# V weights loaded in two halves, a V sum split around transposes, and a tiny early read: the opening of an attention + GLU kernel

## Chip, cores and metric

One core of one Trainium2 chip. The metric is the device time of one execution in microseconds (us). A chip of its own was used for each group of experiments, with the kernel before timed beside them; times are compared within a group.

## The reference, cut to what matters

```python
xn = layernorm(x)                       # x: 2048 x 512
qkv = xn @ wqkv                         # 512 x 1536, 32 heads of 16
A = softmax(mask(q k^T / 4)) v @ wo     # causal, window of 256
B = ((xn @ w_gate) * (xn @ w_up)) @ w_down      # 512 -> 1792 -> 512
return x + A + B
```

## The kernel before

The change touches only the opening, before the steady stream of matmuls. `x` arrives in blocks of 128 rows; VectorE takes the statistics and scales a block (`xn`), TensorE transposes it (four 128 x 128 transposes into PSUM), ScalarE copies it to `xnT`, and four matmuls over the four parts of the 512 input rows make V for the block (`proj_v`). The first K/Q matmul follows when V is made for four blocks.

```python
for lo, hi in ((0, 1), (1, 2), (2, 4)):                 # x blocks 0, 1, 2-3
    nc.sync.dma_start(out=self.x[:, lo:hi, :], in_=xv[:, lo:hi, :])
for lo in (1024, 512, 0):                               # weights of V, K, Q
    nc.sync.dma_start(out=self.Wqkv[:, :, lo:lo + 512], in_=wq[:, :, lo:lo + 512])
# ... gate, up, down and output weights, the rest of x ...
self.keep_busy(40)                                      # filler matmuls, on zeros
# ... first_chunk():
self.norm_transpose(0, False)
self.keep_busy(8)
for b in range(4):
    if b < 3:
        self.norm_transpose(b + 1, False)
    self.proj_v(b, engine="act" if b == 2 else "dve")
    if b == 0:
        self.norm_apply(3)                              # scale block 3
self.proj_qk(0, 0, 1, engine="dve")                     # the first K/Q matmuls
```

The softmax here doesn't subtract the row's maximum and nothing guards it: scores larger than these inputs give would overflow.

## Time and profile before

| | |
|---|---|
| time, median of the first 3 runs | 264.87 us (264.74 to 264.91) |
| the run whose profile was taken | 265.39 us, span 263.7 us |
| TensorE busy | 259.4 us, 98% of the span |
| first V sum / first K/Q matmul | 7.26 / 11.35 us from the span's start |

The chain of work that ended last, as shares of the span, first by engine and then by line:

```profile
PE 96%; DMA 2%; SPq 0%; issue 0%; DVE 0%
PE gp L395 19%; PE up L406 19%; PE psd L428 17%; PE qkp L251 11%; PE S L312 10%; PE acc L366 6%; PE vp L239 5%; PE psd L434 5%; PE L L428 2%; DMA Wqkv<-in_A_wqkv_dram 2%; PE L L434 1%; PE L L366 0%; SPq L74 0%; PE xTp L209 0%; DVE x L444 0%
```

Everything on it is TensorE's work, but for 2% on the load of the V weights.

### The profile page before, as it was taken

The numbers are of one execution on the slowest core, as the hardware profiler recorded it, in microseconds if no ns is written. First come the engines' busy times: TensorE is split into PE (matmuls) and PEld (weight loads), VectorE is DVE, ScalarE is ACT, GpSimd is POOL, SyncE is SP. The second block draws the span as 40 slices with busy tenths as digits, with TensorE's granted clock in tenths as the row PEclk, the third lists the DMA queues.
The fourth block names the chain that finished last, engine by engine and source line by source line (L and its number), as shares of the span: only waits on it lengthen the run. The fifth ranks groups of instructions, "written<-read, shape, count | busy, mean of one in ns | idle before, by whom it ended". The sixth has DMA issues, their size and how long they took to land.

```text
span 263.7 us, 8896 instructions
## 1 busy us (share of the span) xinstructions
PE 259.4 (98%) x3890; PEld 120.9 (46%) x3890; DVE 175.1 (66%) x342; ACT 175.5 (67%) x141; POOL 116.9 (44%) x278
## 2 busy tenths in 40 slices
PE   8999999999999999999999999999999999999996
PEld 8444444444444544444544454444544445444453
DVE  6677888877845497567873669766685135977344
ACT  3376788888856866677776566767777546787600
POOL 6216342425457645334456644544453451463600
PEclk9999999999999999999999999999999999999999
DMA  6999921220002600002001310000100100000002
GB/s 180 378 357 340 281 29 22 24 47 4 0 25 57 84 2 0 4 0 47 5 0 42 81 45 2 0 2 19 32 4 0 42 21 22 5 0 2 4 2 80
DMA packets 19431, 15.12 MB, mean 57 GB/s; under 512 B 7360, under 2 KB 19392, under 8 KB 19392
## 3 DMA queue, kind: packets, MB, share of 16 engines
q1 hardware_dynamic: 18848, 14.26, 19.9%
q8 instruction: 30, 0.49, 0.8%
q10 hardware_dynamic: 544, 0.30, 0.4%
q14 instruction: 9, 0.07, 0.1%
HBM read 9.70 MB, written 2.10 MB: 45 GB/s over the span
## 4 chain that ended last, share of the span: by engine, by line
PE 96%; DMA 2%; SPq 0%; issue 0%; DVE 0%
PE gp L395 19%; PE up L406 19%; PE psd L428 17%; PE qkp L251 11%; PE S L312 10%; PE acc L366 6%; PE vp L239 5%; PE psd L434 5%; PE L L428 2%; DMA Wqkv<-in_A_wqkv_dram 2%; PE L L434 1%; PE L L366 0%; SPq L74 0%; PE xTp L209 0%; DVE x L444 0%
## 5 line engine op out<-in xcount | busy, mean ns | idle before, releaser
L319 ACT ACTIVATE P<-S 128x2048 bf16<-128x2048 f32 x75 | 140.7, 1876 | 50.6 <-PE S L312 46.8
L158 POOL TENSOR_SCALAR_AFFINE_SELECT P<-P 64x256 bf16<-64x256 bf16 x224 | 100.9, 450 | 126.3 <-ACT P L319 112.1
L395 PE MATMUL gp<-xnT,Wg 128*128 128x512 bf16 x224 | 60.1, 380 | 0.0
L406 PE MATMUL up<-xnT,Wu 128*128 128x512 bf16 x224 | 59.1, 380 | 0.0
L411 DVE TENSOR_TENSOR hT<-up,gsb 128x512 bf16<-128x512 f32 x56 | 38.3, 685 | 19.3 <-PE up L406 13.7
L428 PE MATMUL psd<-Wd,hT 128*128 128x512 bf16 (+1 forms) x210 | 48.0, 369 | 0.0
L343 DVE TENSOR_TENSOR P<-P,diag 128x512 bf16<-128x512 bf16 (+1 forms) x75 | 29.4, 392 | 6.1 <-ACT P L319 6.1
L428 PEld LDWEIGHTS <-hT 128*128 128x128 bf16 x238 | 21.3, 98 | 25.1 <-issue 2.9
L406 PEld LDWEIGHTS <-Wu 128*128 128x128 bf16 x224 | 20.5, 98 | 25.4 <-issue 2.5
L395 PEld LDWEIGHTS <-Wg 128*128 128x128 bf16 x224 | 20.3, 98 | 25.1 <-issue 1.9
L312 PE MATMUL S<-Q,K 16*64 16x320 bf16 (+4 forms) x720 | 31.0, 260 | 0.0
L312 PE MATMUL S<-Q,Ko 32*64 32x320 bf16 (+4 forms) x720 | 30.9, 260 | 0.0
L251 PE MATMUL qkp<-xnT,Wqkv 128*128 128x512 bf16 x128 | 29.9, 380 | 0.0
L230 ACT ACTIVATE gsb<-gp 128x512 bf16<-128x512 f32 x39 | 22.9, 596 | 8.2 <-PE gp L395 7.4
L312 PEld LDWEIGHTS <-K 16*64 16x64 bf16 x720 | 12.1, 103 | 30.7 <-issue 30.7
L372 DVE STREAM_TRANSPOSE at<-acc 128x512 f32<-128x512 f32 x30 | 19.1, 688 | 8.9 <-PE acc L366 8.9
L444 DVE TENSOR_TENSOR x<-psd,x 128x512 bf16<-128x512 f32 (+1 forms) x15 | 9.7, 655 | 15.7 <-PE psd L434 15.7
L251 PEld LDWEIGHTS <-Wqkv 128*128 128x128 bf16 x128 | 11.7, 98 | 14.5 <-issue 1.6
L366 PE MATMUL acc<-P,VS 64*32 64x320 bf16 (+4 forms) x672 | 17.7, 253 | 0.0
L366 PE MATMUL acc<-P,V 64*32 64x320 bf16 (+4 forms) x672 | 17.5, 253 | 0.0
L366 PEld LDWEIGHTS <-V 64*32 64x32 bf16 x720 | 15.1, 91 | 2.2 <-issue 1.6
L239 PE MATMUL vp<-Wqkv,xnT 128*128 128x512 bf16 x64 | 15.3, 380 | 0.5 <-DMA Wqkv<-in_A_wqkv_dram 0.5
(54 smaller groups left out, 200.2 us busy)
## 6 DMA issues: line engine op xcount, KB each, us to landing
out_dram<-x SPq DMA_DIRECT2D x15, 128.0 KB, 1.7
Wg<-in_B_w_gate_dram SPq DMA_DIRECT2D x2, 896.0 KB, 11.4
Wu<-in_B_w_up_dram SPq DMA_DIRECT2D x2, 896.0 KB, 13.7
Wd<-in_B_w_down_dram SPq DMA_DIRECT2D x1, 1792.0 KB, 17.2
Wqkv<-in_A_wqkv_dram SPq DMA_DIRECT2D x3, 512.0 KB, 5.9
x<-in_A_x_dram SPq DMA_DIRECT2D x2, 512.0 KB, 8.7
VS<-V SPq DMA_DIRECT2D x6, 144.0 KB, 2.6
x<-in_A_x_dram SPq DMA_DIRECT2D x3, 256.0 KB, 6.6
```

Source lines behind the costliest of these rows:

```text
L158: nc.gpsimd.affine_select(out=v, in_=v, pattern=pattern + [[1 if diag else -1, 64]], compare_op=ALU.is_ge if diag else ALU.is_gt, fill=0.0 ...
L230: nc.scalar.activation(out=out, in_=in_, func=ACT.Copy)
L239: nc.tensor.matmul(ps[:], lhsT=self.xnT[T][:, b, k, :], rhs=self.Wqkv[:, k, 1024:1536], start=(k == 0), stop=(k == 3))
L251: nc.tensor.matmul(ps[:], lhsT=self.Wqkv[:, k, lo:lo + 128], rhs=self.xnT[T][:, :, k, :], start=(k == 0), stop=(k == 3))
L312: nc.tensor.matmul(S[64 * par:64 * par + 64, e, col:col + n], lhsT=(self.Ko if par else self.K)[U, c][rows, keys], rhs=self.Q[T, c][rows, ...
L319: nc.scalar.activation(out=P[:, :, 0:col], in_=S[:, :, 0:col], func=ACT.Exp, scale=0.25)
L343: self.nc.vector.tensor_tensor(out=v, in0=v, op=ALU.min, in1=self.diag.unsqueeze(1).unsqueeze(1).to_broadcast([128, 4, n, 64]))
L366: nc.tensor.matmul(accs[par][32 * e:32 * e + 32, q:q + n], lhsT=v, rhs=P[rows, e, col:col + n], start=(i == 0), stop=(i == len(todo) - 1), ...
L395: nc.tensor.matmul(ps[:], lhsT=self.Wg[:, k, 128 * f:128 * f + 128], rhs=self.xnT[T][:, :, k, :], start=(k == 0), stop=(k == 3))
L406: nc.tensor.matmul(ps[:], lhsT=self.Wu[:, k, 128 * f:128 * f + 128], rhs=self.xnT[T][:, :, k, :], start=(k == 0), stop=(k == 3))
L411: nc.vector.tensor_tensor(out=self.hT[T, f][:], in0=ps[:], in1=self.gsb[:], op=ALU.mult)
L428: nc.tensor.matmul(ps, lhsT=self.hT[T, f][:, 128 * b:128 * b + 128], rhs=self.Wd[:, f, c0:c1], start=(f == 0), stop=False)
```

## The change

Its intent is to shorten TensorE's wait for the V weights: load them in two halves of input rows, begin block 0's sum with the first half, put block 1's transposes between its halves (`self.cur` holds the PSUM tile of the open sum), and touch the weights early with a 16 x 32 read. Two loads of later x blocks are merged with a third, and block 3 is scaled earlier.

```diff
-        for lo in (1024, 512, 0):
-            nc.sync.dma_start(out=self.Wqkv[:, :, lo:lo + 512], in_=wq[:, :, lo:lo + 512])
+        for lo, ks in ((1024, slice(0, 2)), (1024, slice(2, 4)), (512, slice(0, 4)), (0, slice(0, 4))):
+            nc.sync.dma_start(out=self.Wqkv[:, ks, lo:lo + 512], in_=wq[:, ks, lo:lo + 512])
-        for lo, hi in ((8, 10), (10, 12), (12, NT)):
+        for lo, hi in ((8, NT),):
+        first = const.tile([16, 32], BF16, name="first")
+        nc.scalar.dma_start(out=first[:], in_=self.w_d["qkv"][0:16, 1024:1056])
-        (nc.gpsimd if t else nc.vector).tensor_scalar(out=ve[:], ...
+        (nc.vector if t in (0, 3) else nc.gpsimd).tensor_scalar(out=ve[:], ...
-        for b in range(4):
-            if b < 3:
-                self.norm_transpose(b + 1, False)
-            self.proj_v(b, engine="act" if b == 2 else "dve")
-            if b == 0:
-                self.norm_apply(3)
+        self.proj_v(0, (0, 1))
+        first = self.cur
+        self.norm_transpose(1, False)
+        self.cur = first
+        self.proj_v(0, (2, 3), engine="act")
+        self.norm_apply(3)
+        self.proj_v(1, (0, 1))
+        self.norm_transpose(2, False)
+        self.proj_v(1, (2, 3), engine="dve")
+        self.norm_transpose(3, False)
+        self.proj_v(2, engine="act")
+        self.proj_v(3, engine="dve")
```

More of the change, by code (lines that the diff above doesn't have):

```diff
@@ L178, in norm_scale @@
         ve = self.small.tile([128, n], F32, tag="ve", name="ve")
-        (nc.gpsimd if t else nc.vector).tensor_scalar(out=ve[:], in0=mv[:, :, 1], scalar1=1e-5, scalar2=None,
+        (nc.vector if t in (0, 3) else nc.gpsimd).tensor_scalar(out=ve[:], in0=mv[:, :, 1], scalar1=1e-5, scalar2=None,
                                                       op0=ALU.add)
```

## The prediction

> **What bounds the kernel now.** I read the page's busy table first, then what TensorE waited for, then the chain that ended last over its first 12 us, then the timeline of single engines there.
>
> The busy table:
> ```profile
> PE 259.4 (98%) x3890; PEld 120.9 (46%) x3890; DVE 175.1 (66%) x342; ACT 175.5 (67%) x141; POOL 116.9 (44%) x278
> ```
> TensorE is busy for 259.4 of 263.7 us; the next engine has 67%. So TensorE's own work sets the time, and only idle time of TensorE can be won. All the waits of TensorE's matmuls in the whole span:
> ```profile
> PE wps L127 <- DVE idle L94: 1.1, 1, 1.1
> PE vp L239 <- DMA Wqkv<-in_A_wqkv_dram: 0.5, 1, 0.5
> ```
> There are two. The first is the start of the program. The second is the first V projection (`proj_v` of block 0), waiting for the V weights. After that, measured in the stretch 11.51 to 255 us, TensorE is busy 243.49 of 243.49 us. So whatever moves the first K/Q projection (the end of the opening) moves the end by as much, and nothing later can absorb it. The chain over the opening:
> ```profile
> 2.17 4.96 DMA Wqkv<-in_A_wqkv_dram
> 7.12 0.14 issue
> 7.26 1.02 PE vp L239 x4
> 8.28 0.22 PE xTp L209 x4
> 8.50 0.88 PE vp L239 x4
> 9.38 0.01 issue
> 9.39 0.40 PE xTp L209 x4
> 9.79 1.73 PE vp L239 x8
> 11.51 2.59 PE qkp L251 x12
> ```
> The load of the V weights (512 KB, 128 partitions) lands at 7.12 and TensorE goes on at 7.26. Then comes work without a gap, but for one small thing: the transposes of block 3 start at 9.39 while block 1's sum starts at 8.34 and needs 4 x 0.216 = 0.86 us of issue, so they could have started at 9.20. The reader sees the reason in two timeline lines: the block was scaled on VectorE only after the copy of V block 0.
> ```profile
> 8.93 0.40 DVE L190 TENSOR_SCALAR xn<-x,mv,rs 128x512 bf16<-128x512 bf16 x1
> 9.38 0.23 PEld L209 LDWEIGHTS <-xn 128*128 128x128 bf16 x4 [0.51 <-DVE xn L190]
> ```
> The last view is what else stands before the first V sum, TensorE and ScalarE:
> ```profile
> 5.74 0.76 PE L127 MATMUL wps<-idle 128*128 128x128 bf16 x8
> 6.35 0.40 PE L209 MATMUL xTp<-ident,xn 128*128 128x128 bf16 x4
> ```
> ```profile
> 5.77 0.66 ACT L210 ACTIVATE xnT<-xTp 128x256 bf16<-128x256 bf16 x2 [3.48 <-PE xTp L209]
> 6.78 0.60 ACT L210 ACTIVATE xnT<-xTp 128x512 bf16<-128x512 bf16 x1 [0.36 <-PE xTp L209]
> 9.82 0.60 ACT L210 ACTIVATE xnT<-xTp 128x512 bf16<-128x512 bf16 x1 [0.69 <-PE xTp L209]
> ```
> The 8 filler matmuls end their issue at 6.35. Block 0's transposed input is in SBUF in two pieces, at about 6.15 and 6.43. So, but for its weights, the first V sum could start at 6.35. The second ACT line is a cost that the present order hides: from the start of a block's transposes (6.35) to its copy (6.78) are 0.43 us, the copy takes 0.60, and from its end to the matmul that reads it pass some 0.05 us. That is **1.08 us from the start of a block's transposes to its V sum**. Before, block 1's round trip lies wholly under the wait for the weights.
>
> **What the Trainium skill says.** "DMA: Bandwidth & Descriptors", section "Why a DMA increments its semaphore by 16 and not by 1": each engine that takes part counts only after its own data, and only the full 16 means that all has landed. The trace agrees: of the V weights' 16 semaphore packets the first starts at 5.74, most by 6.26, the last at 6.74, and the landing is at 7.12; one slow engine holds the whole load. Same page, "Issuing engines are not separate DMA queues": transfers issued by ScalarE and SyncE share the same 16 engines and interleave. So the tiny read can't have a path of its own; before, no ScalarE transfer exists in the opening, so no run here shows it yet. "TensorE: Matmul & The Clock Gate", section "Wait — 56ns, not 53.3ns?": 215.7 ns from start to start for 512 columns at full clock and 55.6 for 128. The trace agrees: four V matmuls plus the next step take 8.118 - 7.257 = 0.861 us, and the four transposes 8.118 to 8.341 = 0.223.
>
> **The change part by part.**
>
> *Order.* Added TensorE work is nil: the same 16 V matmuls and 16 transposes, in the order V0 (rows 0, 1), transposes 1, V0 (rows 2, 3), V1 half, transposes 2, V1 half, transposes 3, V2, V3. After the opening the order of instructions is the same as before on every compute engine.
>
> *Half of the weights.* A half is 16 KB for each DMA engine instead of 32, in packets of 1 KB whose median is 46 ns. So each engine counts about 16 x 0.046 = 0.74 us earlier: the slowest at some 6.0 instead of 6.74, landing near 7.12 - 0.74 = 6.4, or sooner if the straggler's stall lay in the second half (the typical engine would count by 5.5, landing by 5.9). With the 0.14 us from landing to matmul, the first V sum starts between 6.35 (where the fillers hold it) and 6.54.
>
> *Tiny read.* In the packets the first ones of each load on an engine are slow: 0.25 us for x, up to 0.75 us around 4.3 us where the first of the V weights come, against 46 ns; the four-to-five stretch moves 176 GB/s against 388 in seven-to-eight. I take the intent to be to pay the weights' first access early. It can take up to about 0.5 us off the landing of the first half. But past 6.2 us of landing this wins nothing, since fillers and transposes then hold. Its price is 16 packets of 64 bytes on the engines that fetch x block 0, on which all the normalisation hangs (landed 2.87, statistics from 2.90). I put 0.05 us of delay there.
>
> *Sum, with the first V sum at t0 = 6.35.*
> - V0 half: 2 x 0.216 = 0.43, so transposes 1 start at 6.78 (0.43 later than before).
> - Transposes 1 take 0.22; V0's second half runs 7.00 to 7.44 if its weights have landed by about 6.9. Landed as late as before it runs 7.26 to 7.69, still hidden by the next step.
> - V1's first half needs block 1's copy: 6.78 + 1.08 = 7.86. So TensorE waits about 0.4 us here: the old wait comes back in part, on ScalarE.
> - V1 half to 8.29, transposes 2 from 8.29 to 8.51, V1's other half to 8.94, transposes 3 to 9.17. Block 3's scaling now needs no V copy and should end near 8.4, so the 0.18 us are gone.
> - V2 needs block 2's copy: 8.29 + 1.08 = 9.37 (ScalarE's copy of V0, about 7.9 to 8.5, is out of its way), so 0.2 us of wait. V2 and V3 take 8 x 0.216 = 1.73, to 11.10.
>
> K/Q starts at t0 + 4.75 = 11.10 instead of 11.35: **0.25 us won**. Adding 0.05 for x and 0.05 for a t0 between 6.35 and 6.54 leaves 0.15 to 0.2. So the half's earlier start of up to 0.9 us (7.26 to 6.35) is mostly given back, since block 1's transposes, which used to fill the wait, now stand behind half a sum and bring their round trip to light.
>
> *The rest.* The merged x load and the split of the weights keep the number of loads, and change only which earlier load a later one waits for; gate weights land at 12.49 and are used at 19.18, so nothing comes of it.
>
> **The rivals.**
> 1. *The tiny read holds up x block 0.* For: all share 16 engines, and the first access to the weights was the slowest seen (0.75 us). If it stands ahead of x on each engine and blocks, x lands up to 0.5 us later and every step moves: 264.87 - 0.25 + 0.5 = 265.1. Against: 64 bytes an engine, issued beside x and not before it.
> 2. *The first half lands no earlier than about 6.6*, because a stalled engine is late whatever its share. The break-even is t0 = 11.35 - 4.75 = 6.60; then the time stays at 264.87. For: the landing's tail (6.26 to 6.74) is made of stalls, not of bytes.
> 3. *The tiny read also speeds up x* (its first packets, 0.25 us, may be a start cost of the engines): up to 0.2 us more, 264.4. Against: nothing in the trace shows x waiting for more than its own first access.
> 4. *A large win of 0.9 us*, the whole wait gone and T3's delay too: 263.9. Against it is the 1.08 us round trip, which occurs twice on the new path (blocks 1 and 2).
>
> **Range and chances.** 264.87 - 0.2 = 264.65 us. The three runs of before lie within 0.17 us. Rival 1 gives the upper end, rival 3 with noise the lower: 264.25 to 265.0. A change of 2% is 5.3 us, while the whole opening holds 0.5 us of wait plus 0.18 us of late transposes, and a loss of 5 us would need something to break in a stretch whose order is the same. So within 2% has 0.99.
>
> **What would show it right or wrong.** Right: the first V sum starts near 6.4 with two matmuls, the V weights are gone from TensorE's waits and one for ScalarE's copy of block 1 of 0.2 to 0.4 us stands there; block 3's scaling ends before 8.6; the first K/Q matmul starts near 11.1 to 11.2; the rest of the timeline is moved by that difference. The tiny read's part shows in x block 0's landing (2.87 before) and in the packets around 4 us. Wrong: x lands after 3.1; the first V sum still waits for weights past 6.6; a load's new wait delays gate weights or the blocks of chunk 1; or K/Q starts well before 11.0, which would mean that the round trip is shorter than read here.

## The result, and the profile after

| | before | after |
|---|---|---|
| median of 6 runs | 264.85 us (264.73 to 265.43) | 265.25 us (264.74 to 265.44) |
| ratio after to before | | 1.0009, 95% interval 0.9995 to 1.0022 |
| the profiled run | 265.39 us | 265.20 us |
| first V sum / first K/Q | 7.26 / 11.35 us | 6.38 / 11.14 us |

A ratio here is the mean time of one kernel's fast runs over that of the other's of the same rounds, so it is not quite the ratio of the medians. Executions over 1.5% slower than the fastest of the same kernel are left out of the means. The class is "same"; a small loss is likelier than the gain of 0.2 us that was forecast, and 265.25 lies above the forecast range (264.25 to 265.0). Yet the two *profiles* differ as forecast: K/Q starts 0.21 us sooner. The busy line and the chain of the changed kernel:

```profile
PE 257.6 (98%) x3872; PEld 120.9 (46%) x3890; DVE 174.7 (66%) x342; ACT 176.0 (67%) x142; POOL 116.4 (44%) x277
...
PE 98%; issue 1%; ACT 0%; DVE 0%
```

The DMA share has gone from the chain. TensorE's busy time seems to fall by 1.8 us, but so does the count of its matmuls, by 18, while the count of weight loads is 3890 in both: those are records missing from the trace, not work saved. Profiles with all 3890 records (split2, split4) have none of the "issue" waits of the lines psd, vp and L below, so these come of the missing records too. What TensorE waited for in the changed kernel (line, cause, us in total, times, longest):

```profile
PE psd L436 <- issue: 1.1, 7, 0.2
PE wps L129 <- DVE idle L96: 1.1, 1, 1.1
PE vp L241 <- ACT xnT L212: 0.3, 1, 0.3
PE vp L241 <- issue: 0.2, 1, 0.2
PE L L436 <- issue: 0.2, 1, 0.2
```

The wait for the weights is replaced by one for ScalarE's copy of block 1, as forecast. Its timeline on TensorE and on ScalarE:

```profile
5.74 0.80 PE L129 MATMUL wps<-idle 128*128 128x128 bf16 x8
6.38 0.38 PE L241 MATMUL vp<-Wqkv,xnT 128*128 128x512 bf16 x1
6.81 0.39 PE L211 MATMUL xTp<-ident,xn 128*128 128x128 bf16 x4
7.03 0.59 PE L241 MATMUL vp<-Wqkv,xnT 128*128 128x512 bf16 x2
7.89 0.60 PE L241 MATMUL vp<-Wqkv,xnT 128*128 128x512 bf16 x2 [0.26 <-ACT xnT L212]
8.33 0.39 PE L211 MATMUL xTp<-ident,xn 128*128 128x128 bf16 x4
...
9.40 1.90 PE L241 MATMUL vp<-Wqkv,xnT 128*128 128x512 bf16 x8
11.14 2.75 PE L253 MATMUL qkp<-xnT,Wqkv 128*128 128x512 bf16 x12
```

```profile
7.23 0.60 ACT L212 ACTIVATE xnT<-xTp 128x512 bf16<-128x512 bf16 x1 [0.81 <-PE xTp L211]
```

From block 1's transposes (6.81) to its V sum (7.89) are the 1.08 us of the forecast; from t0 = 6.38 to K/Q (11.14) are 4.76 us against 4.75 forecast. So the mechanism of the forecast stood in this run (block 3's scaling ended at 8.62, a hair after the 8.6 named, and held nothing up), and the time did not follow. Either the profile of before was not of a typical run, or the gain was lost after the opening. The second is soon excluded: the last matmul starts 249.47 us after the first K/Q in both profiles (260.82 - 11.35 and 260.61 - 11.14), with no wait but the missing records. In nearly all later profiles, too, the time of the profiled run is the start of K/Q plus 254.0 to 254.2 us; the exceptions are few_fill (255.0) and both looks at split4 (254.3), and they are taken up below. So, but for these, **K/Q's start can be read for the time.** This also leaves nothing for the merged x load to explain, which was not tested alone.

### The profile page after: what moved, and what is told of

Same layout as the page of the kernel before. It is cut to its first block, busy times and chain, and to the rows that moved or that the text cites. A ratio compares the mean times of both kernels' runs of the same rounds, so it can differ in the third digit from the quotient of the medians.

```text
span 263.5 us, 8878 instructions
## 1 busy us (share of the span) xinstructions
PE 257.6 (98%) x3872; PEld 120.9 (46%) x3890; DVE 174.7 (66%) x342; ACT 176.0 (67%) x142; POOL 116.4 (44%) x277
## 4 chain that ended last, share of the span: by engine, by line
PE 98%; issue 1%; ACT 0%; DVE 0%
PE gp L403 19%; PE up L414 19%; PE psd L436 17%; PE qkp L253 11%; PE S L320 10%; PE acc L374 6%; PE vp L241 5%; PE psd L442 5%; PE L L436 2%; PE wps L129 2%; PE L L442 1%; PE xTp L211 0%; PE L L374 0%; ACT xnT L212 0%; DVE x L452 0%
## 5 line engine op out<-in xcount | busy, mean ns | idle before, releaser
L436 PE MATMUL psd<-Wd,hT 128*128 128x512 bf16 (+1 forms) x198 | 46.1, 368 | 1.4 <-issue 1.1
```

What stands on the lines that cost most here:

```text
L436: nc.tensor.matmul(ps, lhsT=self.hT[T, f][:, 128 * b:128 * b + 128], rhs=self.Wd[:, f, c0:c1], start=(f == 0), stop=False)
```

## The experiments

In each, an expectation stood before the run. The theories: **D**, the spread of run times comes from when the V weights land; **C**, it comes from when TensorE's clock is granted in full; **L**, the change pays only if weights are late; **B**, splitting a load delays its end; **F**, a loss through instruction fetches.

### b1 and b2: the kernel before again

No edit.

> The kernel before again, to see whether its profile above (span 263.7 us, run of 265.4 us) shows a typical run: five of its other six runs took 264.73 to 264.91 us, and one 265.43. Theory D (late DMA): the spread between about 264.8 and 265.4 comes from the landing of the V weights; a run of 264.8 us then has them landed near 6.5 us instead of 7.12 and its first K/Q matmul near 10.8 instead of 11.35. Theory C (clock): the spread comes from when TensorE's clock is granted in full (6.04 us in the profile above); a run of 264.8 us then has it at 5 us or sooner with the V weights still landing near 7.1. If this profile is again of a run of 265.4 us, it shows only that the landing repeats.

> A third look at the kernel before. If a landing of the V weights at 7.1 us is the exception that made the first profiled run take 265.4, this one has it at 6.4 to 6.8, K/Q at 10.7 to 10.95 and takes 264.7 to 265.0. If it again takes 265.3 or more, its K/Q starts near 11.35 with a landing near 7.1 or a clock granted later than 6.8 us.

Measured: b1 264.89 us (264.83 to 264.96; the kernel before beside it 264.95, 264.67 to 265.09 in 11 runs), b2 264.84 us. V weights landed at 6.57 and 6.45 us, K/Q at 10.88 and 10.75. TensorE's matmuls on b1:

```profile
5.74 0.99 PE L127 MATMUL wps<-idle 128*128 128x128 bf16 x8
6.57 0.39 PE L209 MATMUL xTp<-ident,xn 128*128 128x128 bf16 x4
6.79 1.03 PE L239 MATMUL vp<-Wqkv,xnT 128*128 128x512 bf16 x3
```

and on b2:

```profile
5.46 0.61 PE L127 MATMUL wps<-idle 128*128 128x128 bf16 x8
6.42 0.40 PE L209 MATMUL xTp<-ident,xn 128*128 128x128 bf16 x4 [0.34 <-DVE xn L190]
6.65 1.03 PE L239 MATMUL vp<-Wqkv,xnT 128*128 128x512 bf16 x3
```

Neither has a wait for the V weights at all. The chain of b2 in the opening, in order of time, shows what bounds a run whose clock comes early (4.79 us): VectorE's statistics and scaling of block 1, then its transposes.

```profile
5.17 0.61 DVE st L169
5.79 0.02 issue
5.81 0.18 DVE mv L170
5.99 0.38 DVE xn L190
6.37 0.05 issue
6.42 0.40 PE xTp L209 x4
```

So theory D holds for the first profile: its landing at 7.12 us was an exception, and it is the reason why that run took 265.39 us. The wait which the change attacks does not exist in the runs that make the median. Theory C is not dead, though. The 8 fillers took 0.61 us in b2 and 0.99 in b1, and in b1 their end, not VectorE, released block 1's transposes (they start at 6.57 instead of 6.42). The list of runs hints at C as well: of the 38 timed runs of the kernel before beside the experiments, the eight whose mean clock is listed as 0.999 took 265.06 to 265.22 us, the other thirty 264.65 to 265.11, and the one profiled run with 0.999, split2b, got its full clock late (6.74). That the clock makes this smaller spread is not shown.

### a1 and a2: the changed kernel again

No edit.

> The changed kernel again. Its profile (run of 265.2 us) starts the first V sum at 6.38 and K/Q at 11.14 with the clock granted at 6.13 us; two of its six runs took 264.74 and 264.80. Theory C: in a run of about 264.75 us the clock is granted before 5.3 us, the fillers and the transposes of block 0 run at full speed, and K/Q starts near 10.7. Theory D: the weights land at the same times in both kinds of run, since they land before they are needed (5.15 and 5.80 in the profile), so the spread of this kernel can't be the landing of the V weights. On the same chip as the kernel before I expect this one between 0.1 us faster and 0.4 us slower in the mean.

> A third look at the changed kernel. K/Q at the later of t0 + 4.75 and the second half's landing + 3.81; t0 is 5.98 with an early clock, 6.38 to 6.58 with a late one. So K/Q between 10.75 and 11.35, and a time of K/Q + 254.05 (from 264.96 and 10.92): 264.8 to 265.4.

Measured: a1 265.05 us (264.93 to 265.32), ratio 1.0006 (0.9994 to 1.0018); a2 265.15 us. K/Q at 10.92 and 11.07. With the clock granted early (4.28 and 4.95 us) the first V sum started at 5.98 and 5.99, but then the *second* half of the weights was late (7.20 and 7.36). Of the waits of a1, the two that no missing record made and that lie after the start:

```profile
PE vp L241 <- DMA Wqkv<-in_A_wqkv_dram: 0.4, 1, 0.4
PE xTp L211 <- DVE xn L192: 0.2, 1, 0.2
```

Theory D was wrong for this kernel in the form ("they land before they are needed"): its second half does hold it. The two bounds are t0 + 4.75 and the start of V0's second half + 3.67 (0.43 + 0.43 + 1.08 + 1.73): 7.24 + 3.67 = 10.91 for a1 and 7.40 + 3.67 = 11.07 for a2, as measured.

### noread: the change without the tiny read

```diff
-        first = const.tile([16, 32], BF16, name="first")
-        nc.scalar.dma_start(out=first[:], in_=self.w_d["qkv"][0:16, 1024:1056])
```

> The changed kernel without ScalarE's tiny read. If the read is what brought the V weights in early (second half landed at 5.80 against 7.12 us before), then without it the first half lands near 6.2 to 6.4 and the second near 7.1, V0's second half waits until 7.2, and K/Q stays near 11.1, since block 1's round trip through ScalarE ends the wait anyway: time within 0.15 us of the changed kernel. x block 0 lands near 2.87 instead of 2.99. If instead the split or chance brought them in early, the halves land near 5.2 and 5.8 here too.

Measured: 265.40 us (264.99 to 266.29), ratio 1.0021 (1.0009 to 1.0033). Halves landed at 6.13 and 7.41, x block 0 at 2.91. The fillers ran at half speed to their end (8 in 1.01 us), t0 was 6.58 and K/Q came at 11.34 = t0 + 4.76. The profiled run is thus explained without the read. The expectation of a time within 0.15 us of the changed kernel was missed (265.40 against a1's 265.05). Whether the runs are slower than the changed kernel's because of the read is left open: the two intervals overlap.

### order_old: the change's loads with the old order

```diff
-        self.proj_v(0, (0, 1))
-        # ... V0 and V1 in halves around the transposes of blocks 1, 2 ...
+        self.norm_apply(3)
+        for b in range(4):
+            if b < 3:
+                self.norm_transpose(b + 1, False)
+            self.proj_v(b, engine="act" if b == 2 else "dve")
```

> The changed kernel with its loads and its tiny read, but V0's sum whole and behind block 1's transposes as before (block 3 still scaled before V0's copy). If the V weights land by 5.8 us as in the changed kernel's profile, the transposes of block 1 start at 6.4, the first V sum at 6.6 without a wait for ScalarE, and K/Q at 10.5 to 10.6: 0.5 to 0.6 us before the changed kernel's 11.14 and the time 0.5 us less, near 264.3 to 264.8. If the early landing was chance and they land near 7.1, K/Q starts near 11.2, as in the kernel before less the 0.18 us of block 3.

Measured: 265.05 us (264.98 to 265.59), ratio 1.0010 (0.9998 to 1.0022); the hoped-for 0.5 us did not come. The second half landed at 7.84, V0's second half waited 0.55 us for it, and K/Q started at 11.35. The early landing of the first profile after (6.50) was not the rule: of nine profiles with two loads one other (few_fill, 6.58) came near it.

### b_late and a_late: weights made late on purpose

The load of x blocks 4 to 7 (512 KB) goes ahead of the V weights, in both kernels.

```diff
+        nc.sync.dma_start(out=self.x[:, 4:8, :], in_=xv[:, 4:8, :])
         for lo in (1024, 512, 0):        # a_late: the four loads of the change
         # ... in the loop over the gate and up weights, further down:
-            if lo == 0:
-                nc.sync.dma_start(out=self.x[:, 4:8, :], in_=xv[:, 4:8, :])
```

> The kernel before with the load of x blocks 4 to 7 (512 KB) moved ahead of the V weights, so that these land late in every run. Theory L (the change pays only when the V weights are late): from the profiles, K/Q in the kernel before starts 4.23 us after the landing of the V weights if these are what the first V sum waits for (7.12 gave 11.35). 512 KB at 380 GB/s are 1.4 us, so they land at 8.0 to 8.5, K/Q starts at 12.2 to 12.8, and the run takes 1.3 to 1.9 us more than the kernel before on the same chip. A rival, that the time before does not hang on the weights at all, says no change.

> The changed kernel with the same 512 KB ahead of the V weights. Theory L: K/Q starts at the later of t0 + 4.75 (t0 the start of the first V sum) and the landing of the second half + 3.81 (0.14 to the matmul, 0.43 V0's second half, 0.43 V1's first half, 1.08 block 2's round trip, 1.73 V2 and V3). With the second half landing at 8.0 to 8.8 that is 11.8 to 12.6, so about 0.4 us before the other late kernel if both have the same landing, and the run is 0.2 to 0.5 us faster than it. If the change is no better here either, the split itself (more stragglers, a later landing) costs what it saves.

Measured: b_late 269.05 us (266.51 to 269.96), ratio 1.0141 (1.0090 to 1.0193); a_late 267.06 us (266.03 to 270.18, the last one the slow run), ratio 1.0069 (1.0047 to 1.0091), beside 264.80 for the kernel before. The expected sizes were missed. The mean clock listed for each run tells much of the reason: three of b_late's four runs have 0.987 to 0.994 (3.41 us at half clock, as in the profile below, take 0.006 off the mean), and only 266.51 has 1.000; a_late's three runs at 1.000 took 266.03, 266.67 and 267.44. At an equal clock there is no gain from the change to be seen, though one run against three is little. The profiles say more. In b_late the weights landed at 8.83 and the first V sum started at 8.96, but K/Q only at 14.54, 1.5 us later than landing + 4.23. The stretches of TensorE below (length, us busy, number, granted clock, DMA share, GB/s) show why:

```profile
6.66:10.07 3.41, 1.46 (x15) 1.00 1.03 345
10.07:13.48 3.41, 3.41 (x15) 0.50 1.06 389
13.48:16.89 3.41, 3.41 (x17) 1.00 1.08 386
```

TensorE was busy for 1.46 of 3.41 us, and in the next 3.41 us its clock was halved. This is what the Trainium skill describes ("TensorE: Matmul & The Clock Gate", "What's actually happening"): the clock depends on how busy windows of some 3.4 us were, and the windows do not start with the kernel. The trace agrees to the hundredth: 3.41 us. In a_late TensorE stood idle for longer, 2.65 us at a stretch against 1.95, and kept its clock: the grant began at 4.11 there, so the wait fell into two windows, busy for 1.64 us (4.11 to 7.52) and 2.14 us (7.52 to 10.93).

In a_late the first half landed at 8.46 and the second at 9.56. K/Q started at 13.36, where landing + 3.81 says 13.37. But the split had cost more than it saved: with a landing at 8.83 and no loss of clock the old order would have reached 8.83 + 4.23 = 13.06. Theory L is not borne out: as far as these runs show, the lead of the late changed kernel is that of a clock which it happened to keep.

### few_fill: 3 fillers instead of 8 in the changed kernel

```diff
-        self.keep_busy(8)
+        self.keep_busy(3)
```

> The changed kernel with 3 filler matmuls instead of 8 between block 0's transposes and its first V sum. In the four profiles of this order the sum started at 6.38, 5.98, 6.58 and (old order) later, whenever the fillers were through: 107 ns each until the clock is granted in full, 56 after. Theory C (clock): the fillers hold t0; without five of them t0 is 6.2 (ScalarE's first piece at 6.15), K/Q starts near 10.95 to 11.0 whatever the clock does, 0.15 to 0.4 us sooner than in the runs with a late clock, and the time is 0.1 to 0.3 us less than the changed kernel's, with the second half of the weights as the next bound (landing + 3.81). Rival: fewer fillers leave TensorE less busy, the clock is granted later, V runs at half speed (0.43 us a matmul), and K/Q comes at 11.3 or later.

Measured: t0 6.21 and K/Q 10.98, as theory C said. But the time was 265.97 us (265.64 to 266.34), ratio 1.0041 (1.0029 to 1.0054): 1.1 us *more* than the kernel before, where 0.1 to 0.3 less than the changed kernel was expected. The opening was right; the loss is at 189 us. The chain there, first in this run:

```profile
187.50 1.68 PE acc L374 x123
189.19 0.62 issue
189.81 0.74 PE acc L374 x31
```

"issue" is time in which the engine waited for nothing that the profile shows. With its lost pace around it, the piece costs 0.92 us: the last matmul came 250.39 us after K/Q. The trace has a 16 KB packet on the instruction queue starting at 187.2 us here, and at 185.3 us in the changed kernel. Such packets are most likely TensorE's own instructions: the kernel before has 30 of them on this queue for 3890 matmuls and 3890 weight loads, some 259 for each packet (an estimate from these counts).

### fill_moved: the five fillers moved, not dropped

```diff
-        self.keep_busy(8)
+        self.keep_busy(3)
         # ... V0 ...
         self.norm_apply(3)
+        self.keep_busy(5)
         self.proj_v(1, (0, 1))
```

> The run with 3 fillers started K/Q at 10.98, as theory C said, but lost 0.9 us at 188 us, in the middle of a sum over values, where TensorE stood without a wait that the profile shows while its own instructions were being fetched: 16 KB of them[...] were asked for at 187.2 us there, and at 185.3 in the changed kernel. Theory F (fetch): with 10 instructions less ahead of it the border between two fetches moved into a stretch of short instructions. Here the five fillers are not dropped but moved behind V0's sum, where TensorE waits for block 1's copy, so all later instructions keep their places. Theory F expects no stall at 188 us, K/Q at 10.95 to 11.0, the last matmul 249.47 us after it as in the other profiles, and a time of 264.7 to 264.95, 1 us under the run with 3 fillers. If the loss has another cause (fewer fillers as such), it stays at 265.6 or more.

Measured: the same stretch of the chain is whole again:

```profile
187.85 2.40 PE acc L375 x175
190.25 0.33 PE S L321 x9
```

and the last matmul starts 249.47 us after K/Q. The stall went away with the five fillers back in place, which is what theory F says. "Runtime: NRT & Kernel Launch", "Instruction fetch mechanics", of the Trainium skill states refills in blocks of 16 KiB, 256 instructions, mostly hidden; the packets agree with the size, and if the stall was a fetch, it was not hidden here. That the fetch is the cause fits, but was not isolated: few_fill's packet took 1.43 us and was over at 188.6, before the stall began at 189.19, and what happened between is not in the trace. The time, 265.36 us (265.15 to 266.01), ratio 1.0022 (1.0009 to 1.0036), missed the expectation for another reason, the one that a1 has: the second half landed at 7.34, V0's second half started at 7.38 and the moved fillers queued behind it, so K/Q started at 11.33.

### b_read: the tiny read alone

```diff
+        first = const.tile([16, 32], BF16, name="first")
+        nc.scalar.dma_start(out=first[:], in_=self.w_d["qkv"][0:16, 1024:1056])
```

> The kernel before with the tiny read alone. If the read brings the V weights in earlier, they land before 6.5 us (6.57 and 7.12 in the two profiles without it), and the first V sum starts at 6.6 to 6.8, where fillers and block 1's transposes hold it anyway: time equal to a typical run of the kernel before (264.9) and no run near 265.4. If the read delays x and with it everything, x block 0 lands 0.05 to 0.1 us later than 2.87 to 2.90 but block 0's transposes still start at 5.31 behind the fillers, so no loss shows either. A slower time by 0.1 us or more would say that the read costs something on the path.

Measured: 264.83 us (264.81 to 265.69), ratio 1.0005 (0.9991 to 1.0018). Weights at 6.49, x block 0 at 2.91, K/Q at 10.72. The read neither helps nor harms, within this noise; one run of the five took 265.69 us, where none near 265.4 was expected, and it has no profile. Over all profiles x block 0 landed at 2.81 to 2.99 with it and at 2.80 to 3.02 without.

### order_only: the new order alone

```diff
-        for b in range(4):
-            # ... transposes of block b + 1, then the V sum of block b ...
+        self.proj_v(0, (0, 1))
+        # ... as in the change; one load of the V weights, no tiny read ...
```

> The kernel before with the changed order alone: V0 in two halves around block 1's transposes and block 3 scaled early, but one load of the V weights and no tiny read. Both halves of V0 then start only when all V weights have landed (6.5 to 7.1, so t0 6.65 to 7.25), and block 1's transposes and their round trip of 1.08 us stand behind that. K/Q at t0 + 4.75 = 11.4 to 12.0 against 10.89 in the typical profile of the kernel before: 0.5 to 0.9 us slower, 265.4 to 265.8. If the order costs nothing, the time is that of the kernel before.

The earlier scaling of block 3 is in this run too. Measured: 265.82 us (265.59 to 266.17) against 264.77 beside it, ratio 1.0039 (1.0026 to 1.0052): of the parts tested by themselves (order, split, read) the only one with a clear effect, and it is a loss of 1.0 us. The whole change loses some 0.2 us, so its other parts buy most of this back; the profiles point to the early first half, with t0 at 5.98 to 6.58 against 6.59 here. The weights were there at 6.29; what the order costs is no wait for them:

```profile
6.59 0.59 PE L239 MATMUL vp<-Wqkv,xnT 128*128 128x512 bf16 x1
7.23 0.39 PE L209 MATMUL xTp<-ident,xn 128*128 128x128 bf16 x4
...
8.31 0.61 PE L239 MATMUL vp<-Wqkv,xnT 128*128 128x512 bf16 x2 [0.26 <-ACT xnT L210]
```

Half a sum ahead of block 1's transposes took 0.64 us instead of 0.43, since the clock was still at half for most of it, and from 7.23 to 8.31 the round trip of 1.08 us runs in full view. K/Q came at 11.57.

### split2 and split4: the split alone

```diff
-        for lo in (1024, 512, 0):
+        for lo, ks in ((1024, slice(0, 2)), (1024, slice(2, 4)), (512, slice(0, 4)), (0, slice(0, 4))):
```

split4 has four loads of the V weights in the same way. Both keep the old order and have no tiny read.

> The kernel before, in its own order and without the tiny read, with the V weights in two loads. Theory B: the second half lands at 7.2 to 7.6, as in the changed order, so V0's third matmul waits until 7.35 to 7.75, K/Q starts at 7.5 + 0.43 + 3.23 = 11.1 to 11.4 instead of 10.75 to 10.89, and the time is 0.3 to 0.6 us above the kernel before. Rival (chance, read or x load): the second half lands at 6.3 to 6.6 and nothing changes, K/Q near 10.7 to 10.9.

> A second look at the split in two: theory B has the second half between 6.8 and 7.8 again, the rival between 6.3 and 6.6 in at least one of the two looks.

> The same with four loads, one for each 128 input rows. Theory B: two more slow starts put the last quarter at 7.8 to 9, V0's last matmul waits for it, and K/Q starts at the last landing + 0.14 + 0.22 + 3.23, 11.4 to 12.6: 0.6 to 1.8 us slower than the kernel before. Rival: no later than one load, no change in time.

> A second look at the split in four: theory B has the last quarter at 7.8 or later again, and later than both looks of the split in two.

Measured: split2 264.99 us (264.91 to 265.78), ratio 1.0011 (0.9998 to 1.0024), second halves at 7.77 and, in the second look (265.17 us), 7.31. split4 265.51 us (265.10 to 266.12), ratio 1.0027 (1.0013 to 1.0041), last quarters at 7.13 and, in the second look (265.08 us), 7.27. The wait of split2 for the second half:

```profile
PE vp L239 <- DMA Wqkv<-in_A_wqkv_dram: 0.5, 1, 0.5
```

The rival falls: without the read and without the merged x load, too, both looks have the V weights end later (7.77, 7.31) than any profile with one load (7.12 at most). But a larger dose does not delay it more: four loads end no later than two (7.13 and 7.27 against 7.31 and 7.77), so "a slow start for every load" is not the explanation. Nor is it that SyncE issues the second half later (at 2.68 us, the single load at 2.17): of the 16 engines that share a load, the eighth to finish does so at 5.8 to 6.3 us for the second half, in the nine profiles with two loads, and at 6.1 to 6.5 for the single load. Only the last ones are late: the sixteenth comes 0.4 to 1.8 us after the eighth, against 0.2 to 0.6. Why the last engines of a split load are late stays open.

Note also that the profiled run of split2 took 0.65 us more than its median, and that three of its five runs took 264.91 to 264.99, as the kernel before: the wait above is that of a slow draw, and the split alone costs no clear time.

Neither look at split4 waits for weights, with K/Q at 10.83 and 10.75, but both were of runs well under its median of 265.51, so why this is 0.5 us up is open too. A part lies at the other end: from the last matmul's start to the end of the span are 3.13 us in both, and 2.85 to 2.99 in all other profiles.

### All profiles side by side

Times in us from the span's start. "Clock" is the first record of the full clock; with a tilde it is taken from where the starts of 128-column matmuls fall from 107 to 56 ns apart (in order_only from the 0.64 us of the half sum). (The page's row of clocks and the clock column of a stretch are no help for the opening: there is no record before the first grant, and they print full clock there.)

| profile | V weights landed | clock | first V sum | K/Q | that run |
|---|---|---|---|---|---|
| before, first | 7.12 | 6.04 | 7.26 | 11.35 | 265.39 |
| b1 | 6.57 | ~6.5 | 6.79 | 10.88 | 264.96 |
| b2 | 6.45 | 4.79 | 6.65 | 10.75 | 264.84 |
| b_read | 6.49 | 3.71 | 6.63 | 10.72 | 264.89 |
| order_only | 6.29 | ~7.0 | 6.59 | 11.57 | 265.59 |
| after, first | 5.80, 6.50 | 6.13 | 6.38 | 11.14 | 265.20 |
| a1 | 5.56, 7.20 | 4.28 | 5.98 | 10.92 | 264.96 |
| a2 | 5.44, 7.36 | 4.95 | 5.99 | 11.07 | 265.15 |
| noread | 6.13, 7.41 | ~6.5 | 6.58 | 11.34 | 265.43 |
| order_old | 5.39, 7.84 | ~6.8 | 6.95 | 11.35 | 265.43 |
| few_fill | 5.47, 6.58 | 5.69 | 6.21 | 10.98 | 265.98 (stall) |
| fill_moved | 5.36, 7.34 | 5.67 | 6.21 | 11.33 | 265.39 |
| split2 | 5.35, 7.77 | 5.40 | 6.73 | 11.47 | 265.64 |
| split2b | 5.50, 7.31 | 6.74 | 6.89 | 11.02 | 265.17 |
| split4 (first, last) | 4.97, 7.13 | 3.98 | 6.73 | 10.83 | 265.13 |
| split4b (first, last) | 5.13, 7.27 | 4.03 | 6.61 | 10.75 | 265.08 |

The kernel before in its typical runs has K/Q at 10.75 and 10.88; the changed one at 10.92, 11.07 and 11.14, in the mean 0.23 us later. No version that I tried starts it before 10.72, and none beats the kernel before.

## Why the prediction was right or wrong, point by point

**"The sum, with the first V sum at t0 = 6.35": right.** t0 + 4.75 gave K/Q to 0.02 us in the two runs that it bounds (first after, noread), and the round trip of 1.08 us was found where it was put. The second half "still hidden by the next step" if it landed at 7.12 was also right: with t0 at 6.35 even the 7.20 and 7.36 of a1 and a2 would have stayed hidden (they bound K/Q to 10.91 and 11.07, under 11.10). There they were in the way because t0 was earlier, 5.98 and 5.99. That t0 came so near to 6.35 in the first profile after (6.38) was luck: its clock was granted at 6.13, nearly as in the profile before (6.04). Rival 4, the large win, fell with the round trip.

**"K/Q starts at t0 + 4.75 = 11.10 instead of 11.35: 0.25 us won": the failing step is the 11.35.** It came from a profile of a run of 265.39 us and was subtracted from a median of 264.87. The typical run starts K/Q at 10.75 to 10.88 (b1, b2), because its V weights land at 6.45 to 6.57 and are not waited for. With the right starting point the same sum gives 11.10 - 10.82 = +0.28 us: a small loss. The page showed the wait in plain sight, but the table of times beside it said that the run was not typical, by as much as the wait was long.

**"Half of the weights" was mis-sized.** The first half came as early as forecast or earlier (5.4 to 6.1 against 5.9 to 6.4). The cost was left out: the second half landed at 6.50 to 7.84 (middle of nine profiles with two loads 7.34), while one load lands whole at 6.29 to 7.12 (middle of five 6.49), a_late and b_late not counted. The lines of the prediction hold a slip here too: in the profile before two engines, not one, held the landing (they count at 7.11 and 7.12 us, the next one at 6.76).

**Where the fillers "hold" the sum: right in kind, too firm in size.** 6.35 was for a clock granted at 6.04. Over the profiles of the changed order with 8 fillers and weights in halves t0 was 5.98 to 6.58, as the clock was granted early or late. The kernel before depends on this less, for VectorE (6.42) stands right behind its fillers.

**"Tiny read": both the feared delay (rival 1) and the hoped gain (rival 3) are nil** within what the landings of x block 0 resolve, some 0.1 us; the 0.05 us that I put down can't be told from nothing. I had taken the slow first packets for a price of the first access; the read does not remove the late landings.

**Rival 2** named the right quantity (a stalled engine is late whatever its share) but for the first half; it is the second half that is late.

**Chances:** within 2% with 0.99 was right and not in doubt, since the opening holds less than 1 us.

Not settled: why a split load ends late on its last engine; split4's median; what makes the spread of the kernel before below 265.3 us; and whether noread's runs are slower than the changed kernel's for a reason other than the clock.

## What to carry to other kernels

Before forecasting from a wait in a profile, compare that run's own time with the median: a wait as long as the excess may be an accident of that run, as it was here, and removing it then wins nothing in the median. Profile the kernel a second time first. The rule holds for experiments too, as split2 shows. An idle wait is a place where other work may hide; moving work into it can bring the round trip of what stood there (here 1.08 us through PSUM and ScalarE) onto the path, so test the new order alone. And read the clock off the spacing of the matmuls in an opening: what is moved ahead of its grant runs at half speed.

## What the Trainium skill lacked or had wrong

- "TensorE: Matmul & The Clock Gate", "What you observe", has the change to full clock at about 4 us of sustained work, give or take 0.5 us from run to run. Here, with fillers from 1.07 us on in every run, it came at 3.71 to about 7.0 us, so 2.6 to 5.9 us after the start.
- "DMA: Bandwidth & Descriptors", "Rules for kernel authors", advises large loads but no page says that splitting one can delay its end: 512 KB landed at 6.29 to 7.12 us as one load and at 6.50 to 7.84 as two, with the first half at 5.35 to 6.13.
- "Runtime: NRT & Kernel Launch", "Instruction fetch mechanics", calls crossing a 16 KiB block mostly hidden. With ten instructions fewer ahead of it a stretch of short matmuls lost 0.92 us, and none when they were put back. If this was a fetch, as argued but not isolated above, it was not hidden; that instruction counts can move such a stall is on no page.
